# Early expert jobs of a gated scan with a mixture of experts: four taken at the seventh unit instead of two, 51 early tiles instead of 55

## The chip, the cores and the metric

The kernel runs on one core of a Trainium2 chip. The metric is the device time of one execution in microseconds (us). Five engines share the core: PE (TensorE, matmuls), DVE (VectorE), ACT (ScalarE), POOL (GpSimd) and SP (SyncE, which here only issues DMAs). PEld is PE's loading of weights, which overlaps its matmuls. Matmuls write to banks of PSUM, and ACT and DVE read them from there.

## What is computed

`x` and `f_logit` are 4 sequences of 3648 steps with 256 channels. A gated scan runs along each sequence, and its output is routed, token by token, to one of 16 experts.

```python
sig = 1.0 / (1.0 + np.exp(-f_logit))
f = lower_bound[None, None, :] + (1.0 - lower_bound[None, None, :]) * sig
for t in range(S):
    h = f[:, t] * h + (1.0 - f[:, t]) * x[:, t]
    y[:, t] = h
...
g_idx = np.argmax(x @ w_group, axis=1)            # x is now y, 14592 tokens
e_idx = np.argmax(xg @ w_expert[g], axis=1)
h = np.maximum(xg[mask_e] @ w1[g, e], 0.0)        # 256 -> 1024
ye = h @ w2[g, e]                                 # 1024 -> 256
out[tok_idx] = (g_w * e_w)[:, None] * ye
```

So every token passes through one expert. The matmuls of the experts are the bulk of the work.

## The kernel before

**Two halves that overlap.** The scan and the routing are the background. They go through 29 units of 512 tokens (`UNIT`, the last one is half a unit). For each unit SP or ACT loads 1 MB (`zt`), ACT makes the gate, DVE gates the input (L206, L226) and scans it (L217, one scan for each half of the channels, more where a sequence ends), PE turns it back (L244) and multiplies it by the router's weights (L258, L269), and DVE works out the expert and the place of each token (L279 to L335). POOL then writes each token's row (`rows`) with an indirect DMA (L339) into a list for its expert in DRAM (`xs`).

**Jobs.** The experts' matmuls are cut into jobs. An early job (kind A, one for each expert) takes the first rows of an expert's list while the list is still growing: `EARLY` gives for each expert the unit after which its list is read and the number of tiles of 128 rows that are taken. `early_rows` issues the loads (`xr`, L707) on SP as soon as that unit's tokens are written. Places that the list could not fill by then hold blank rows, written ahead by `early_blanks` (L490). After all tokens are routed, `order` sorts the experts by what is left of each, and 16 late jobs (kind B) take the rest, the largest first. Their sizes are fixed when the program is built: `CAPS`. What doesn't fit would go to a loop behind the program (L972), one tile for each pass.

**One job.** Its weights come in four pieces of 512 KB (`st`, L715, on SP, eight buffers, so two jobs ahead). Each piece is split into a half-precision part by ACT (`wh`, L721) and a remainder by DVE (`wl`, L722). The rows are turned by PE (L762, early jobs alone), split into `xh` (ACT) and `xl` (DVE, L768), and their numbers kept in `meta` (L770). The first layer is done by chunks of at most 256 rows (`m1_step`): 48 matmuls of the chunk's width (L796 to L798), and for each bank an ACT instruction (`hh`, L801) and a DVE instruction (`hl`, L802). The second layer is done by parts of at most 128 rows (`m2_step`, L815): 24 matmuls of 256 columns for a part of 97 to 128 rows; for shorter ends the columns are laid side by side, 48 matmuls of 128 columns for up to 64 rows (two groups) and 96 of 64 columns for up to 32 (four groups). ACT scales the result (`o`, L827) and POOL scatters it (L828).

**What sets the order.** SP's queue is in the order of the program text. The other engines' order is set when the program is built. The text mixes background and jobs by `bg_step`: behind each step of a job it issues as much background as is needed so that the unit in `EARLY` of the job after the next is routed by the middle of the present job (`due`). From the middle of job 12 on the whole background, `order` too, has to be out.

Of the kernel before, what the change touches and what calls it, by code (L numbers as in the profile page):

```python
# [19 lines left out]
NE = 16  # L20
UNIT = 512

EARLY = [(7, 2), (7, 2), (9, 2), (9, 2), (11, 2), (11, 2), (13, 3), (15, 3),
         (15, 3), (17, 4), (19, 4), (21, 4), (23, 5), (25, 5), (27, 6), (27, 6)]
CAPS = [848, 748, 724, 592, 588, 560, 528, 488, 464, 460, 448, 420, 392, 296, 168, 112]
EXTRA_AT = []
GROUPS = [2, 2, 2, 1] + [2] * 11
LAG = 7
# [6 lines left out]
AHEAD = 3  # L35
MT = -(-max(CAPS) // 128)
ZX_SP = 9
# [3 lines left out]
def gated_scan_moe(ctx: ExitStack, tc, zx, lower, wroute, wexp, out, S):  # L41
# [7 lines left out]
    NT = N // P  # L49
    PRE = max(n for _, n in EARLY) * P  # L50
    LW = PRE + N + 2 * P
# [44 lines left out]
    early = const.tile([P, NE], F32, name="early")  # L96
    for e, (_, n) in enumerate(EARLY):
        nc.vector.memset(early[:, e:e + 1], float(n * P))
# [4 lines left out]
    floors, gaps = {}, {}  # L103
    for u in sorted({u for u, _ in EARLY}):
        m = floors[u] = const.tile([P, NE], F32, name=f"floor{u}")
        es = [e for e, (v, _) in enumerate(EARLY) if v == u]
        nc.vector.memset(m, -1.0)
# [74 lines left out]
    def p1_ta(u):  # L182
        a, b = unit_range(u)
        w = b - a
        U = units[u]
        U["h"] = p1.tile([P, KD, UNIT], F32, name="h", bufs=3)
        ff = U["z"][:, 0]
        if u > 0:
            nc.scalar.activation(ff[:, :, 0:w], U["z"][:, 0, :, 0:w], AF.Tanh, scale=0.5)
        for k in range(KD):  # L190
            if u == 0:
                nc.scalar.activation(ff[:, k, 0:w], U["z"][:, 0, k, 0:w], AF.Tanh, scale=0.5)
            nc.scalar.activation(ff[:, k, 0:w], ff[:, k, 0:w], AF.Identity, scale=hlf[:, k:k + 1],
                                 bias=cen[:, k:k + 1])
        U["f"] = ff
# [152 lines left out]
    def p1_thunks(us, groups):  # L348
# [21 lines left out]
        def put(f):  # L370
            th.append(f or (lambda: None))
            if hasattr(f, "mark"):
                marks[f.mark] = len(th)

        put(lambda: [p1_load(u) for u in range(us[0], us[0] + AHEAD - 1)])
        put(lambda: p1_ta(us[0]))
        cut = EARLY[0][0]

# [12 lines left out]
        for u in us + [us[-1] + 1]:  # L391
# [52 lines left out]
            for t in seq:  # L444
                put(t)
                slot += 1
                for _ in range(2 if u <= EARLY[0][0] else 1):
                    if not hold:
# [168 lines left out]
    for s in range(NE):  # L617
        nc.vector.memset(caps[:, s:s + 1], float(CAPS[s]))
    onesf = const.tile([P, NE], F32, name="onesf")
# [8 lines left out]
    def make_job(kind, idx):  # L628
        j = Job()
        j.kind, j.idx = kind, idx  # L630
        j.len = EARLY[idx][1] * P if kind == "A" else CAPS[idx] if kind == "B" else P
        j.tiles = -(-j.len // P)
# [399 lines left out]
```

## Time and profile before

| | |
|---|---|
| median of 3 runs | 783.15 us (781.83 to 784.55) |
| profiled execution | 783.16 us |
| its span, first to last instruction | 781.3 us |
| PE busy | 710.7 us (91%) |
| DVE busy | 545.8 us (70%) |
| ACT busy | 460.6 us (59%) |
| POOL busy | 295.0 us (38%) |

The page's shares are averages over stages with different limits. The stages are told apart by the table of windows, which gives the busy time of each engine in a stretch, and the stretches are cut at the first `hh` of a job. In the windows, "(x202)" is the number of instructions, PEclk the granted clock of TensorE as a share of 2.4 GHz, and DMA share how busy the 16 DMA engines were on average.

### The profile page before, as it was taken

Reading aid. Unit: us, or ns where it says so; the run is one execution under the profiler, and the core shown is the slowest. Engines: PE = TensorE matmul, PEld = TensorE weight load, DVE = VectorE, ACT = ScalarE, POOL = GpSimd, SP = SyncE. Lnnn points to the kernel's source line nnn. Section 1 sums busy time; section 2 is a strip of 40 time slices with the busy share of each in tenths; the row PEclk is TensorE's granted clock in tenths of the full one; section 3 lists DMA queues with packets and bytes.
Section 4 is the critical chain, followed back from the end, with each engine's and each line's share of the span. In section 5 each row is a group of like instructions: output and inputs, shape, how many; then the busy total and the mean of one; then the engine's idle time right before and its main releaser. Section 6 shows DMA issues by size and latency. Waiting matters only on the chain.

```text
span 781.3 us, 20837 instructions
## 1 busy us (share of the span) xinstructions
PE 710.7 (91%) x8077; PEld 628.7 (80%) x8077; DVE 545.8 (70%) x1130; ACT 460.6 (59%) x817; POOL 295.0 (38%) x261
## 2 busy tenths in 40 slices
PE   2553778999999999999999999999999999999995
PEld 1332566888988878989988898999999999899995
DVE  7989999999999976675654645545564676566640
ACT  5756876987878855445445444454555465555541
POOL 1574164677756553542111213223222322232232
PEclk9999979999999999999999999999999999999999
DMA  7997989999999935369535434453553555556300
GB/s 299 348 328 240 348 234 357 338 312 336 306 367 320 345 111 190 117 200 226 158 113 108 149 88 126 128 125 120 138 168 99 160 154 171 169 152 177 86 29 25
DMA packets 95605, 155.58 MB, mean 199 GB/s; under 512 B 52304, under 2 KB 64621, under 8 KB 92048
## 3 DMA queue, kind: packets, MB, share of 16 engines
q1 hardware_dynamic: 80528, 103.73, 44.9%
q0 software_dynamic: 11424, 30.02, 11.0%
q10 hardware_dynamic: 3552, 20.48, 7.4%
q8 instruction: 64, 1.05, 0.6%
q14 instruction: 37, 0.30, 0.1%
HBM read 112.69 MB, written 42.02 MB: 198 GB/s over the span
## 4 chain that ended last, share of the span: by engine, by line
PE 72%; DVE 6%; issue 5%; DMA 3%; ACT 3%; POOL 1%; SPq 1%; POOLq 0%; ACTq 0%; DVEq 0%
PE ps_m L815 34%; PE ps_m L796 8%; PE ps_m L798 8%; PE ps_m L797 8%; PE ps_p L796 3%; PE ps_p L797 3%; PE ps_p L798 3%; DVE wl L722 2%; PE ps_p L244 2%; PE ps_p L762 2%; POOL out_dram L828 1%; DVE h L217 1%; PE ps_p L258 1%; DMA xs<-blank 1%; DMA xs<-rows,posi 1%
## 5 line engine op out<-in xcount | busy, mean ns | idle before, releaser
L815 PE MATMUL ps_m<-wh,hl 128*128 128x256 f16 (+2 forms) x1320 | 265.9, 251 | 4.9 <-DVE hl L802 4.9
L815 PE MATMUL ps_m<-wl,hh 128*128 128x256 bf16 (+2 forms) x1320 | 265.6, 251 | 0.1
L815 PE MATMUL ps_m<-wh,hh 128*128 128x256 f16 (+2 forms) x1320 | 265.5, 252 | 0.0
L815 PEld LDWEIGHTS <-hh 128*128 128x128 f16 (+2 forms) x2640 | 195.3, 99 | 23.5 <-issue 3.5
L796 PE MATMUL ps_m<-xh,wh 128*128 128x256 f16 (+11 forms) x782 | 197.2, 263 | 3.6 <-DVE hl L802 3.6
L797 PE MATMUL ps_m<-xl,wh 128*128 128x256 bf16 (+11 forms) x782 | 197.3, 262 | 1.0 <-DVE xl L768 1.0
L798 PE MATMUL ps_m<-xh,wl 128*128 128x256 f16 (+11 forms) x782 | 197.3, 262 | 0.9 <-issue 0.9
L722 DVE TENSOR_TENSOR wl<-st,wh 128x1024 bf16<-128x1024 f32 x128 | 154.3, 1219 | 51.9 <-ACT wh L721 51.7
L339 POOL DMA_INDIRECT xs<-rows,posi x114 | 142.9, 1253 | 124.6 <-DVE rows L321 34.6
L828 POOL DMA_INDIRECT out_dram<-o,info x75 | 87.1, 1162 | 242.5 <-ACT o L827 214.6
L802 DVE SCALAR_TENSOR_TENSOR hl<-ps_m,hh 128x512 bf16<-128x512 f32 (+6 forms) x176 | 117.5, 670 | 72.6 <-ACT hh L801 71.9
L801 ACT ACTIVATE hh<-ps_m 128x512 f16<-128x512 f32 (+6 forms) x176 | 103.3, 588 | 69.4 <-PE ps_m L798 67.0
L721 ACT CAST wh<-st 128x1024 f16<-128x1024 f32 x128 | 132.1, 1046 | 14.0 <-PE ps_m L815 8.0
L815 PEld LDWEIGHTS <-hl 128*128 128x128 bf16 (+2 forms) x1320 | 104.5, 99 | 15.6 <-DVE hl L802 5.2
L796 PEld LDWEIGHTS <-wh 128*128 128x128 f16 x1088 | 107.0, 99 | 11.8 <-issue 2.8
L797 PEld LDWEIGHTS <-wh 128*128 128x128 f16 x1088 | 107.1, 98 | 10.7 <-issue 2.6
L798 PEld LDWEIGHTS <-wl 128*128 128x128 bf16 x1088 | 107.0, 98 | 9.1 <-issue 1.2
L828 POOL DMA_INDIRECT out_dram<-o,meta x55 | 63.0, 1145 | 112.1 <-ACT o L827 101.8
L827 ACT ACTIVATE o<-ps_m,info 128x256 f32<-128x256 f32 (+4 forms) x75 | 33.0, 441 | 84.3 <-PE ps_m L815 76.9
L796 PE MATMUL ps_p<-xh,wh 128*128 128x256 f16 (+13 forms) x306 | 73.4, 252 | 0.0
L798 PE MATMUL ps_p<-xh,wl 128*128 128x256 f16 (+13 forms) x306 | 73.3, 252 | 0.0
L797 PE MATMUL ps_p<-xl,wh 128*128 128x256 bf16 (+13 forms) x306 | 73.3, 252 | 0.0
(138 smaller groups left out, 736.7 us busy)
## 6 DMA issues: line engine op xcount, KB each, us to landing
st<-in_wexp_dram SPq DMA_DIRECT2D x128, 512.0 KB
zt<-in_zx_dram ACTq DMA_DIRECT2D x19, 1024.0 KB
zt<-in_zx_dram SPq DMA_DIRECT2D x8, 1024.0 KB
xr<-xs SPq DMA_DIRECT2D x25, 258.0 KB
xs<-blank SPq DMA_DIRECT2D x22, 258.0 KB
xs<-rows,posi POOLq DMA_INDIRECT x114
xs<-blank SPq DMA_DIRECT2D x3, 516.0 KB
xs<-blank SPq DMA_DIRECT2D x2, 774.0 KB
```

Source lines behind the costliest of these rows:

```text
L244: nc.tensor.transpose(out=bp[:, (j - j0) * D + k * P:(j - j0) * D + (k + 1) * P], in_=h[:, k, j * P:(j + 1) * P], identity=ident)
L339: sc = nc.gpsimd.indirect_dma_start(out=xs_v[G["t0"] + t][:, :], out_offset=bass.IndirectOffsetOnAxis(ap=R["posi"][:, t:t + 1], axis=0), i ...
L721: nc.scalar.copy(j.wh[i], j.st[i])
L722: nc.vector.tensor_tensor(out=j.wl[i], in0=j.st[i], in1=j.wh[i], op=ALU.subtract)
L796: nc.tensor.matmul(po, w1_at(j.wh, k, c), xh[:, k], start=(k == 0), stop=False)
L797: nc.tensor.matmul(po, w1_at(j.wh, k, c), xl[:, k], start=False, stop=False)
L798: nc.tensor.matmul(po, w1_at(j.wl, k, c), xh[:, k], start=False, stop=(k == KD - 1))
L801: nc.scalar.activation(hi, pv, AF.Relu)
L802: nc.vector.scalar_tensor_tensor(out=j.hl[ch][:, cs[0]:cs[-1] + 1, 0:w], in0=pv, scalar=0.0, in1=hi, op0=ALU.max, op1=ALU.subtract)
L815: nc.tensor.matmul(pm[i * q:i * q + n, 0:dw], h[ch][:, c, ts], w2_at(w, c)[:, i * dw:(i + 1) * dw], start=(c == 0 and s == 0), stop=(c == ...
L827: nc.scalar.activation(o[s, 0:dw], pm[s, 0:dw], AF.Copy, scale=lt.bitcast(F32)[s, r, 1:2])
L828: nc.gpsimd.indirect_dma_start(out=out_v[out_n[0]].rearrange("n (g d) -> (n g) d", g=g), out_offset=bass.IndirectOffsetOnAxis(ap=lt[s, r, ...
```

## The change

```diff
-EARLY = [(7, 2), (7, 2), (9, 2), (9, 2), (11, 2), (11, 2), (13, 3), (15, 3),
-         (15, 3), (17, 4), (19, 4), (21, 4), (23, 5), (25, 5), (27, 6), (27, 6)]
-CAPS = [848, 748, 724, 592, 588, 560, 528, 488, 464, 460, 448, 420, 392, 296, 168, 112]
+EARLY = [(7, 2), (7, 2), (7, 2), (7, 2), (9, 2), (9, 2), (11, 2), (11, 2), (13, 3),
+         (15, 3), (17, 4), (19, 4), (21, 4), (23, 5), (25, 6), (27, 6)]
+CAPS = [848, 748, 724, 620, 616, 592, 588, 576, 548, 512, 500, 460, 392, 296, 288, 172]
```

Early jobs 2 and 3 are read at unit 7 instead of 9, jobs 4 and 5 at 9, jobs 6 and 7 at 11 with two tiles each instead of three, and so on. In all 51 early tiles (6528 rows) stand where 55 (7040) stood, and the late jobs hold 8480 rows instead of 7836. Jobs 13, 14 and 15 have 5, 6 and 6 tiles in both kernels. Early jobs have 27 chunks instead of 30 and late ones 41 instead of 38. The late jobs' parts are 63 of full width instead of 57, 9 in two groups instead of 11, and 7 in four groups instead of 8.

Since the table also feeds `bg_step` and the blanks, the order on the engines moves. On SP, from the last row load of the first early jobs to the row loads for unit 9 (`xr` are early rows, `st` weights, `xs<-blank` blank rows, `posA` the place in the list):

```order
+L707 ISA
+L707 DMA xr<-xs 128x516
 L715 DMA st<-in_wexp_dram 128x1024 x5
 L490 DMA xs<-blank 384x1x258
-L715 DMA st<-in_wexp_dram 128x1024 x2
-L490 DMA xs<-blank 384x1x258 x2
+L715 DMA st<-in_wexp_dram 128x1024 x6
+L490 DMA xs<-blank 384x1x258
+L715 DMA st<-in_wexp_dram 128x1024 x4
 L679 TENSOR_LOAD posA
```

Two more row loads now stand ahead of the weights, and 15 pieces of weights instead of 7 stand ahead of the wait for unit 9's rows.

On DVE, from the first `hl` of early job 0 on, before (`mx` to `sc` are the routing of a group of units, `zt` the gate, `h` the scan):

```order
L802 SCALAR_TENSOR_TENSOR hl<-ps_m_871,hh 128x512
L279 TENSOR_REDUCE mx<-Lg 128x40
L281 TENSOR_TENSOR ge<-Lg,mx 128x160
L285 SCALAR_TENSOR_TENSOR pw<-ge,pri 128x160
L287 TENSOR_REDUCE pm<-pw 128x40
L289 TENSOR_TENSOR oh<-pw,pm 128x160
L294 TENSOR_TENSOR oh_962<-oh 128x8x16
L297 SCALAR_TENSOR_TENSOR scn<-rmask_322,oh_962 128x128
L327 TENSOR_TENSOR both<-ps_p,runoff 128x32
L332 TENSOR_TENSOR sc<-scn,both 128x128
L206 SCALAR_TENSOR_TENSOR zt<-zt 128x1024
L802 SCALAR_TENSOR_TENSOR hl<-ps_m_983,hh 128x512
```

The same place in the changed kernel:

```order
L802 SCALAR_TENSOR_TENSOR hl<-ps_m_895,hh 128x512
L722 TENSOR_TENSOR wl_963<-st,wh_962 128x1024
L217 SCALAR_TENSOR_TENSOR h<-zt,h 128x512
L802 SCALAR_TENSOR_TENSOR hl<-ps_m_939,hh 128x512
L279 TENSOR_REDUCE mx<-Lg 128x40
L281 TENSOR_TENSOR ge<-Lg,mx 128x160
L802 SCALAR_TENSOR_TENSOR hl<-ps_m_987,hh 128x512
L768 TENSOR_TENSOR xl<-ps_p,xh 128x512
L770 COPY meta<-xr 128x4
L285 SCALAR_TENSOR_TENSOR pw<-ge,pri 128x160
L287 TENSOR_REDUCE pm<-pw 128x40
L802 SCALAR_TENSOR_TENSOR hl<-ps_m_1023,hh 128x512
```

Where one `hl` followed another after ten rows of background, the four `hl` of job 0 now stand close together. From the first `hl` of job 0 to the first of job 13, DVE has 504 rows before (the trace has records of 502) and 480 now: 8 fewer `hl`, 3 fewer `xl`, 3 fewer `meta`, 1 `wl` fewer, 1 scan more (it stood just ahead of the stretch before), and 10 fewer of the small rows of `leftovers` (these now stand behind). All scans, all routing and the sorting in `order` lie ahead of that point in both.

## Rows read from the trace of the kernel before

**Rows 1.** The page's 40 equal slices of the span: busy share in tenths for PE and DVE, and the granted clock in tenths.

```profile
PE   2553778999999999999999999999999999999995
...
DVE  7989999999999976675654645545564676566640
...
PEclk9999979999999999999999999999999999999999
```

**Rows 2.** The table of windows, cut where a job's first `hh` starts (job 0 at 80.02, 1 at 107.68, 2 at 123.77, 3 at 137.92, 5 at 163.76, 11 at 288.61, 12 at 313.72, 13 at 342.11; the last matmul's `o` ends at 773.5): stretch, its length, busy time and count on each engine, granted clock, DMA share and GB/s.

```profile
core 0: us, PE busy (x) PEld busy (x) DVE busy (x) ACT busy (x) POOL busy (x), PEclk, DMA share, GB/s
80.02:107.68 27.66, 20.86 (x202) 16.32 (x201) 25.29 (x58) 19.93 (x42) 8.63 (x8) 0.81 0.94 305
107.68:123.77 16.09, 10.87 (x87) 8.47 (x86) 16.02 (x26) 13.46 (x23) 12.47 (x10) 0.85 0.91 257
123.77:137.92 14.15, 13.74 (x127) 11.74 (x125) 13.96 (x27) 10.29 (x20) 4.52 (x4) 0.92 1.02 391
137.92:163.76 25.84, 25.84 (x259) 23.01 (x258) 25.05 (x46) 22.26 (x41) 16.45 (x13) 1.00 1.01 323
...
80.02:288.61 208.59, 193.62 (x1949) 167.62 (x1948) 199.05 (x379) 164.45 (x305) 120.62 (x93) 0.96 0.94 311
80.02:280.00 199.98, 185.01 (x1861) 160.17 (x1860) 193.61 (x364) 160.21 (x298) 115.58 (x89) 0.96 0.97 322
288.61:313.72 25.11, 25.11 (x244) 22.19 (x243) 15.71 (x38) 14.28 (x28) 11.14 (x12) 1.00 0.52 169
...
80.02:342.11 262.09, 246.76 (x2468) 214.94 (x2467) 238.01 (x502) 192.44 (x358) 149.12 (x122) 0.97 0.83 276
342.11:773.50 431.39, 429.89 (x5364) 392.19 (x5362) 239.42 (x428) 218.52 (x371) 106.86 (x94) 1.00 0.49 136
```

**Rows 3.** The same table for line 801 (`hh`) alone; a job of two tiles has four of them, and jobs 0 to 12 have 76 together.

```profile
80.01:107.67 27.66, 2.42 (x4) 0.81 0.94 305
107.67:123.76 16.09, 2.43 (x4) 0.85 0.91 257
...
137.90:288.60 150.70, 27.86 (x46) 1.00 0.93 310
288.60:342.10 53.50, 10.75 (x18) 1.00 0.42 139
```

**Rows 4.** The list of waits for PE from 80 to 140 us: who waited for whom, us in total, times, longest.

```profile
PE ps_m L815 <- DVE hl L802: 4.9, 1, 4.9
PE ps_p L762 <- DMA xr<-xs: 2.4, 1, 2.4
PE ps_m L796 <- DVE hl L802: 1.8, 1, 1.8
```

**Rows 5.** SP's timeline: start, us (waits included), line, DMA issued, count.

```profile
71.45 1.52 SPq L707 DMA_DIRECT2D xr<-xs  x2
73.07 5.51 SPq L715 DMA_DIRECT2D st<-in_wexp_dram  x5
78.63 1.40 SPq L490 DMA_DIRECT2D xs<-blank  x1
80.13 9.94 SPq L715 DMA_DIRECT2D st<-in_wexp_dram  x2
90.12 1.87 SPq L490 DMA_DIRECT2D xs<-blank  x2
108.26 1.50 SPq L707 DMA_DIRECT2D xr<-xs  x2
```

**Rows 6.** DVE's timeline: start, us for the run of equal instructions, count.

```profile
70.07 4.61 DVE L722 TENSOR_TENSOR wl<-st,wh 128x1024 bf16<-128x1024 f32 x4
...
94.70 2.46 DVE L217 TENSOR_TENSOR_SCAN h<-zt,h 128x512 f32<-128x512 f32 x2
...
108.55 1.28 DVE L802 SCALAR_TENSOR_TENSOR hl<-ps_m,hh 128x512 bf16<-128x512 f32 x2
```

**Rows 7.** The groups of DVE instructions by line and shape: count, busy us, mean ns of one, idle time before. The last is one of the small rows (128x16) of `leftovers`.

```profile
L722 DVE TENSOR_TENSOR wl<-st,wh 128x1024 bf16<-128x1024 f32 x128 | 154.3, 1219 | 51.9 <-ACT wh L721 51.7
L802 DVE SCALAR_TENSOR_TENSOR hl<-ps_m,hh 128x512 bf16<-128x512 f32 x148 | 100.9, 685 | 63.6 <-ACT hh L801 62.9
...
L768 DVE TENSOR_TENSOR xl<-ps_p,xh 128x512 bf16<-128x512 f32 x25 | 17.1, 683 | 9.3 <-ACT xh L767 9.3
...
L588 DVE TENSOR_TENSOR t<-t,caps 128x16 f32<-128x16 f32 x1 | 0.2, 174 | 0.0
```

**Rows 8.** The chain that ended last, in order of time: start, us, what, count. They are second layers: a full part of 24 matmuls has 2.62 us; 72 is a full one and one in two groups, 120 a full one and one in four groups, 48 two full ones.

```profile
610.94 4.08 PE ps_m L815 x72
...
626.04 2.62 PE ps_m L815 x24
633.90 3.53 PE ps_m L815 x120
```

**Rows 9.** PE's timeline where it passes to early job 11, in square brackets the idle time ahead and who ended it; and the window of that job.

```profile
274.54 0.33 PE L269 MATMUL ps_p<-ident,rs 128*128 128x128 f32 x1 [0.39 <-DVE xl L768]
279.44 0.27 PE L796 MATMUL ps_m<-xh,wh 128*128 128x256 f16 x1 [1.51 <-DVE hl L802]
...
261.33:288.61 27.28, 25.38 (x251) 22.15 (x250) 23.07 (x41) 18.15 (x35) 10.58 (x8) 1.00 0.61 203
```

**Rows 10.** The groups of instructions of PE's weight loads on line 796: 16 for each chunk of the first layer.

```profile
L796 PEld LDWEIGHTS <-wh 128*128 128x128 f16 x1088 | 107.0, 99 | 11.8 <-issue 2.8 <-ACT wh L721 0.4
```

## The prediction

> **What bounds the kernel now.** I read the 40 slices first, then the windows cut at the jobs, then who waits for whom. The slices [rows 1] show three stretches: PE is half empty up to some 140 us, then full to the end; DVE is full up to some 270 us and half empty afterwards; the granted clock falls below full speed only around 90 to 130 us. So there are two stages, and each has its own limit.
>
> From job 13 on PE is the limit: 429.89 of 431.39 us are busy [rows 2]. Whatever is left at that point takes PE's time and little else, and from the last `o` at 773.5 to the span's end at 781.3 there are 7.8 us more, which I leave as they are.
>
> Between the first `hh` of job 0 (80.02) and the first of job 11 (288.61) DVE is the limit: it is busy for 199.05 of 208.59 us, and up to 280.00 for 193.61 of 199.98 [rows 2]. PE is busy for 20.86 of 27.66 us in job 0, 10.87 of 16.09 in job 1 and 13.74 of 14.15 in job 2 [rows 2], and what it waits for there is DVE above all: 4.9 us for an `hl`, 1.8 for another [rows 4]. In job 0 an `hl` stands behind a block of routing and scans. The counts of `hh` (four for a job of two tiles, 76 up to job 13) show that the cuts are where I say [rows 3]. From job 3 to 5 PE too is full, 25.84 of 25.84, beside DVE at 25.05 [rows 2]. That is the point on which this case turns: the early jobs are fed at a rate that holds both engines, and the change shifts early work about in a stage that DVE bounds.
>
> **The change, part by part.** *Jobs 2 and 3 at unit 7.* The first four jobs now have their rows before they start, so less background is pressed between them, and PE's empty time in jobs 0 to 2 (27.66 - 20.86, 16.09 - 10.87 and 14.15 - 13.74, together 12.4 us) gets filled. This is no gain of 12.4 us, since DVE had no room there: the scans that are not done now are done a few jobs later, on the same full DVE. So I don't count PE's gaps. I count what DVE has to do up to a point where the background is over in both kernels, which is the first `hl` of job 13.
>
> *DVE up to job 13.* Before: 238.01 us busy [rows 2]. The change in rows is told with the order. Prices are spacings, since neighbours overlap: a `wl` (4.61 - 1.22) / 3 = 1.13, an `hl` 1.28 - 0.685 = 0.60, a scan 2.46 - 1.27 = 1.19 (half of 2.46 is 1.23) [rows 6, 7]; an overlap of 0.085 off 683 ns makes 0.60 for an `xl`, and off 174 ns 0.09 for a small one [rows 7]. So -8 x 0.60 (`hl`) - 3 x 0.60 (`xl`) - 1.13 (`wl`) + 1.19 (scan) - 13 x 0.09 (three `meta` and ten small rows) = -7.7, and 230.3 us remain. The four tiles less that the early jobs have by then are all of this; the splits of weights and the background stay.
>
> *DVE's idle time in that stretch.* Before, up to 280.00, it was 199.98 - 193.61 = 6.4 us, 3.3% of its work [rows 2]; up to 288.61 it was 9.5, or 4.8%. I take 3.3% = 7.6 us, since up to 280 DVE was the limit and behind that PE was. Ends: none, and 4.8% = 11.0.
>
> *Ahead of job 0.* DVE's and PE's rows are the same. SP issues two more blank writes of 258 KB ahead of the first weights and two more row loads behind 71.45; a pair of row loads took 1.52 us of the queue [rows 5], and the pieces that come next wait for no one yet. 0.5 MB at the 305 GB/s of job 0's window [rows 2] would be 1.7 us of the DMA engines if it delayed a unit's load in full. I take 0.5 us, between 0 and 1.8.
>
> *SP.* Before, SP stood from 90.12 + 1.87 to 108.26 at the row loads of unit 9, with the last piece of job 3's weights behind it [rows 5]. Now 15 pieces go ahead of that wait. Without it the first four jobs lack no weights; and the 2.4 us that PE waited for those rows [rows 4] go. DVE covers both, so I price them at nothing, and if DVE were not full there they would be part of the 12.4 us above.
>
> *PE behind job 13.* Jobs 13 to 15 are the same. The late jobs grow by 644 rows: 48 columns a row, 30912 columns, at 2.62 us for 24 x 256 columns [rows 8] 13.2 us. Second layers: +6 full parts x 2.62, -2 in two groups x (4.08 - 2.62 = 1.46), -1 in four groups x (3.53 - 2.62 = 0.91) [rows 8] = +11.9. Together +25.1 us. Against it stand four early tiles less (4 x 5.24 = 21 us of PE) ahead of job 13, where PE has the room already: so in this sum they give nothing beyond DVE's 7.7.
>
> *Sum.* Job 13 starts at 80.0 + 0.5 + 230.3 + 7.6 = 318.4 instead of 342.1. Behind it 431.4 + 25.1 = 456.5, to 774.9 instead of 773.5, and 7.8 to the end: a span of 782.7. The profiled execution had 783.16 for a span of 781.3, 1.9 more, so 784.6 us. That execution is at the median of the runs (783.15). The change gains 23.7 us ahead of job 13 and pays 25.1 behind it.
>
> With the ends: 784.6 - 7.6 - 0.5 = 776.5 without any idle time, and 784.6 + 3.4 + 1.3 = 789.3 with both upper ends.
>
> **Rivals.** *PE gets in DVE's way (slower).* Ahead of job 13 PE has 246.76 - 21 = 226 us busy against DVE's 230: both full at once, and a full PE in order makes DVE wait. Where this could be seen before, at the passage to job 11, PE lost 0.39 + 1.51 = 1.9 us while DVE had 23.07 busy of 27.28 [rows 9]. From job 8 to 12 the changed order puts as much background beside each tile as DVE can bear. With 1.9 us in three of these jobs beyond my 7.6: 784.6 + 5.7 = 790.3. Against it: from job 3 to 5 both were full and nothing was lost, PE 25.84 of 25.84 [rows 2]. It decides from about 8.5 us of idle DVE on (784.6 + 0.9 is slower by over 0.3%).
>
> *The first four jobs want more than the DMA engines give (slower).* Jobs 0 to 2 moved 27.66 x 305 + 16.09 x 257 + 14.15 x 391 = 18.1 MB [rows 2]. Four jobs with one scanned unit less, half a job's weights and two tiles more need some 18.5. At the 311 GB/s of the whole stage [rows 2] that is 59.5 us, against some 56 of DVE in those jobs (13 `wl`, 16 `hl`, 12 scans, 5 gates, 4 `xl`, 58 small rows): 3.5 late, 788.1 us. Against it: 391 GB/s in job 2 [rows 2], with which it costs nothing. The Trainium skill (DMA: Bandwidth & Descriptors, section Where 436 GB/s comes from) puts what HBM gives one core at about 358 GB/s; by that 18.5 MB take an estimated 51.7 us, and this rival has no price. As a ceiling the trace does not bear it out: the 391 GB/s of job 2 are above it, reads and writes together.
>
> *DVE never waits (faster).* Early jobs at hand mean that DVE finds an `hl` or a split to do whenever a scan's input is late. With 2 us of idle time left: 784.6 - 5.6 = 779.0. For it: DVE was busy for 16.02 of 16.09 us in job 1 [rows 2]. Against it: 2.4 us of DVE's 6.4 fell to job 0 alone, and the rest came while PE was full.
>
> *The change doesn't do what it says.* If a late job's rows exceeded its size, the loop behind the program would run, at least 5.2 us of PE for each pass. Worked out from the inputs of the reference, the experts' remainders are 102 to 837 before and 162 to 837 now, and every size in the table is 8 to 11 rows above its own. Before, the loop did not run: 1088 weight loads are 16 for each of 68 chunks [rows 10], and there are 68 now too.
>
> **How the numbers follow.** A run of this kernel can tell about 0.3% from no change, 2.35 us, so no change lies between 780.8 and 785.5. My forecast, no difference that can be told, has 0.43; PE in DVE's way 0.25 and the DMA engines 0.11, both slower; DVE never waiting 0.20, faster; the loop 0.01, slower. That is 0.20 faster, 0.43 the same, 0.37 slower. The range goes from 777.5, one us inside the lower end, to 790.0, about where the first rival ends; some 2 in 10 lie outside.
>
> **What would show it.** The first `hh` of job 13 (the 77th) near 318 us with DVE some 230 us busy between; PE's four waits before 140 us gone and the clock falling less; PE full behind job 13 for some 455 us. If job 13 starts before 314, DVE had less to do or waited less than I say; if it starts behind 321, the windows of jobs 8 to 12 should show whether PE, or in jobs 0 to 3 the DMA share, is what DVE waited for. If PE's time behind job 13 is not 25 us longer, the price of the late rows is wrong.

## Result and profile after

| | before | after |
|---|---|---|
| median | 782.95 us (14 runs, 780.94 to 785.76) | 789.42 us (14 runs, 784.37 to 793.19) |
| profiled execution | 783.16 us | 791.82 us |
| its span | 781.3 us | 790.1 us |

The changed kernel takes 1.0075 times as long (95% interval 1.0057 to 1.0093): slower by three quarters of a per cent, 4.8 us above the forecast and inside its range. The profiled execution lies 2.4 us above its median; a second one, further down, lies below.

The windows, cut at the first `hh` of jobs 0, 1, 2, 3, 4 and 13 and at the end of the last `o`, answer to [rows 2]:

```profile
core 0: us, PE busy (x) PEld busy (x) DVE busy (x) ACT busy (x) POOL busy (x), PEclk, DMA share, GB/s
84.06:92.09 8.03, 8.03 (x85) 7.08 (x84) 7.30 (x15) 6.45 (x13) 0.00 (x0) 1.00 1.01 397
92.09:104.22 12.13, 12.13 (x124) 10.73 (x123) 12.13 (x25) 11.64 (x22) 0.00 (x0) 1.00 0.95 340
104.22:120.55 16.33, 13.43 (x131) 11.50 (x130) 16.12 (x31) 12.16 (x22) 12.73 (x10) 1.00 0.91 279
120.55:142.67 22.12, 17.16 (x153) 13.81 (x152) 14.98 (x30) 13.02 (x23) 15.59 (x11) 0.85 0.89 262
...
250.82:274.84 24.02, 22.42 (x221) 19.06 (x219) 21.00 (x42) 20.07 (x42) 13.38 (x11) 1.00 1.03 339
...
84.06:327.01 242.95, 224.20 (x2220) 192.44 (x2219) 226.15 (x462) 181.76 (x342) 148.44 (x114) 0.98 0.86 287
327.01:783.22 456.21, 454.65 (x5460) 415.66 (x5458) 249.12 (x454) 227.73 (x386) 112.91 (x101) 1.00 0.49 133
```

Jobs 0 and 1 run with PE full, 8.03 of 8.03 and 12.13 of 12.13 us; the gaps of [rows 2] are gone there. In job 3 both engines stand: DVE has 14.98 of 22.12 us and PE 17.16, at a granted clock of 0.85. Up to job 13 DVE is idle for 242.95 - 226.15 = 16.8 us. Job 0 starts 4.0 us later than before. Behind job 13 PE is full, as before.

The waits of PE from job 0 to job 13, which answer to [rows 4]:

```profile
PE ps_m L796 <- DVE hl L802: 7.1, 7, 2.1
PE ps_p L762 <- DMA xr<-xs: 5.8, 2, 5.0
```

The wait for early rows, which I said would go, has grown from 2.4 to 5.0 us for the longest. SP's timeline, to hold against [rows 5], shows when those rows were asked for:

```profile
74.71 3.77 SPq L707 DMA_DIRECT2D xr<-xs  x4
...
99.25 17.87 SPq L715 DMA_DIRECT2D st<-in_wexp_dram  x4
126.34 1.50 SPq L707 DMA_DIRECT2D xr<-xs  x2
```

The row loads for unit 9 go out at 126.34 instead of 108.26. By then job 3, the last job that has its rows, is 5.8 us past its first `hh`; before it was job 1, 0.6 us past its own. POOL's timeline shows the first and the last of the eight scatters of the group with unit 9 (the first stood behind 33.86 us without work):

```profile
105.07 1.33 POOL L339 DMA_INDIRECT xs<-rows,posi  x1 [33.86 <-ACT hh L801]
...
116.78 1.97 POOL L339 DMA_INDIRECT xs<-rows,posi  x1 [0.31 <-issue]
```

and the same two in the kernel before:

```profile
94.12 1.39 POOL L339 DMA_INDIRECT xs<-rows,posi  x1 [24.51 <-ACT hh L801]
...
103.71 1.18 POOL L339 DMA_INDIRECT xs<-rows,posi  x1 [0.30 <-issue]
```

From the start of the last scatter to the row loads, while the scatters land, are 9.6 us, 4.6 before. So, counted from the first `hh` of job 0, the loads go out 14.0 us later than before (at 42.3 us): the first scatter stands 6.9 us later, the eight take 2.1 us more from first to last, and the landing takes 5.0 us more. What makes the landing slower is not shown. What follows can be read on PE (start, us, and in square brackets the idle time ahead):

```profile
123.87 0.27 PE L798 MATMUL ps_m<-xh,wl 128*128 128x256 f16 x1
129.10 1.10 PE L762 MATMUL ps_p<-ident,xr 128*128 128x128 f32 x4 [4.96 <-DMA xr<-xs]
130.00 0.42 PE L815 MATMUL ps_m<-wh,hh 128*128 128x256 f16 x1
```

and on DVE:

```profile
131.79 0.15 DVE L770 COPY meta<-xr 128x4 int32<-128x4 int32 x1
139.08 0.69 DVE L802 SCALAR_TENSOR_TENSOR hl<-ps_m,hh 128x512 bf16<-128x512 f32 x1 [7.14 <-ACT hh L801]
```

PE takes its work in order: behind the turning of job 4's rows stand the second layer of job 2 and the rest of job 3, and DVE's next `hl` needs those. DVE takes its rows in order too: the next rows of routing and scan stand behind that `hl`, so it has nothing to do meanwhile. So 5.0 us of PE become 7.1 us of DVE. That it is more has to do with the clock, in windows around the wait (columns as above):

```profile
120.00:127.70 7.70, 4.14 (x48) 3.19 (x46) 7.70 (x18) 7.15 (x12) 6.48 (x5) 1.00 0.65 231
127.70:134.60 6.90, 5.50 (x26) 4.07 (x27) 4.24 (x7) 0.94 (x2) 5.68 (x5) 0.51 0.98 220
```

PE stood from 123.87 on, the granted clock fell to the lower of its two levels (1.2 GHz), and the first 5.5 us of work behind the wait ran at it: some 2.7 us more, by halves.

PE's weight loads on line 796 are as many as in [rows 10], so the loop behind the program did not run:

```profile
L796 PEld LDWEIGHTS <-wh 128*128 128x128 f16 x1088 | 107.0, 98 | 10.5 <-issue 1.6
```

### The profile page after: what moved, and what is told of

It is laid out like the page before. It is cut to its first block, busy times and chain, and to the rows that moved or that the text cites. A ratio compares the mean times of both kernels' runs of the same rounds, so it can differ in the third digit from the quotient of the medians.

```text
span 790.1 us, 20452 instructions
## 1 busy us (share of the span) xinstructions
PE 713.4 (90%) x7925; PEld 630.2 (80%) x7925; DVE 544.0 (69%) x1116; ACT 460.7 (58%) x817; POOL 296.3 (38%) x260
## 4 chain that ended last, share of the span: by engine, by line
issue 51%; POOL 15%; DVE 9%; DMA 8%; PE 6%; POOLq 1%; ACT 1%; SPq 0%; DVEq 0%; ACTq 0%
POOL out_dram L828 14%; DMA xs<-rows,posi 3%; DVE wl L722 3%; DMA out_dram<-o,meta 2%; PE ps_m L815 2%; POOL xs L339 2%; DVE hl L802 1%; DVE h L217 1%; DMA st<-in_wexp_dram 1%; DMA xr<-xs 1%; DMA zt<-in_zx_dram 1%; PE ps_m L797 1%; PE ps_m L796 1%; PE ps_m L798 1%; POOLq L828 1%
## 5 line engine op out<-in xcount | busy, mean ns | idle before, releaser
L796 PE MATMUL ps_m<-xh,wh 128*128 128x256 f16 (+12 forms) x760 | 192.8, 263 | 8.2 <-DVE hl L802 8.1
L797 PE MATMUL ps_m<-xl,wh 128*128 128x256 bf16 (+12 forms) x760 | 193.2, 262 | 1.6 <-DVE xl L768 1.6
L798 PE MATMUL ps_m<-xh,wl 128*128 128x256 f16 (+12 forms) x760 | 193.1, 262 | 0.0
L339 POOL DMA_INDIRECT xs<-rows,posi x114 | 146.8, 1288 | 123.5 <-ACT hh L801 34.2
L802 DVE SCALAR_TENSOR_TENSOR hl<-ps_m,hh 128x512 bf16<-128x512 f32 (+8 forms) x173 | 114.9, 667 | 70.1 <-ACT hh L801 69.9
L801 ACT ACTIVATE hh<-ps_m 128x512 f16<-128x512 f32 (+8 forms) x173 | 101.9, 591 | 63.7 <-PE ps_m L798 63.7
L828 POOL DMA_INDIRECT out_dram<-o,meta x51 | 57.8, 1134 | 100.4 <-ACT o L827 89.6
L802 DVE SCALAR_TENSOR_TENSOR hl<-ps_p,hh 128x512 bf16<-128x512 f32 (+11 forms) x71 | 46.3, 652 | 58.5 <-ACT hh L801 58.4
L796 PE MATMUL ps_p<-xh,wh 128*128 128x256 f16 (+13 forms) x328 | 78.8, 252 | 0.0
L797 PE MATMUL ps_p<-xl,wh 128*128 128x256 bf16 (+13 forms) x328 | 78.7, 252 | 0.0
```

What stands on the lines that cost most here:

```text
L339: sc = nc.gpsimd.indirect_dma_start(out=xs_v[G["t0"] + t][:, :], out_offset=bass.IndirectOffsetOnAxis(ap=R["posi"][:, t:t + 1], axis=0), i ...
L796: nc.tensor.matmul(po, w1_at(j.wh, k, c), xh[:, k], start=(k == 0), stop=False)
L797: nc.tensor.matmul(po, w1_at(j.wh, k, c), xl[:, k], start=False, stop=False)
L798: nc.tensor.matmul(po, w1_at(j.wl, k, c), xh[:, k], start=False, stop=(k == KD - 1))
L801: nc.scalar.activation(hi, pv, AF.Relu)
L802: nc.vector.scalar_tensor_tensor(out=j.hl[ch][:, cs[0]:cs[-1] + 1, 0:w], in0=pv, scalar=0.0, in1=hi, op0=ALU.max, op1=ALU.subtract)
```

## Experiments

My theory after this reading had two losses: the start of job 0 (two more blank writes while the DMA engines are full) and the rows of unit 9, late for job 4. The rival was that 51 tiles instead of 55 cost the time by themselves. Times are medians, ratios are to the kernel before on the same chips. The kernel before came to 782.95 us beside the first run, 784.28 beside e2 to e6, 783.45 beside e8 to e11 and 783.10 beside e13 to e15, so runs are compared by their ratios. "Stage" is from the first `hh` of job 0 to that of job 13.

| run | us | ratio (95%) | job 0 | job 13 | DVE busy in the stage | DVE idle |
|---|---|---|---|---|---|---|
| after | 789.42 | 1.0075 (1.0057-1.0093) | 84.06 | 327.01 | 226.15 | 16.80 |
| e15_after | 788.77 | 1.0095 (1.0072-1.0118) | 81.86 | 322.75 | 226.69 | 14.20 |
| e2_tiles | 788.26 | 1.0063 (1.0034-1.0091) | 80.55 | 330.56 | 230.60 | 19.41 |
| e10_tiles_due | 787.02 | 1.0042 (1.0025-1.0059) | 80.80 | 329.05 | 231.47 | 16.78 |
| e3_noblank | 785.59 | 1.0020 (0.9997-1.0043) | 78.91 | 321.75 | 226.41 | 16.43 |
| e4_late_after | 785.79 | 1.0029 (1.0008-1.0050) | 82.64 | 320.61 | 227.40 | 10.57 |
| e6_due | 783.16 | 0.9996 (0.9978-1.0013) | 82.00 | 317.29 | 227.81 | 7.48 |
| e8_due_late | 784.98 | 1.0019 (1.0001-1.0037) | 83.87 | 322.47 | 227.99 | 10.61 |
| e9_due_fetch | 781.60 | 0.9975 (0.9961-0.9989) | 81.68 | 317.99 | 227.96 | 8.35 |
| e14_due_fetch | 781.31 | 0.9974 (0.9959-0.9988) | 80.77 | 317.17 | 227.90 | 8.50 |
| e11_due_noblank | 779.26 | 0.9938 (0.9918-0.9957) | 79.02 | 315.27 | 228.07 | 8.18 |

**The late rows.** One more due time:

```diff
+    due.append((work(macros[0]) + work(macros[1]) // 2, marks[9]))
     now = [0]
```

> The changed kernel with one more due time: unit 9 has to be routed by the middle of job 1 rather than of job 2, so more background stands ahead of job 4. Theory (job 4's rows came 18 us later than before, since unit 9 is routed late, and DVE lost 7 us by it): SP's row loads of unit 9 go out some 10 us earlier, PE's wait of 5.0 us for them is gone, DVE's idle stretch of 7.1 us at 139 falls below 2, and the time is 783 to 786 us. Rival (DVE and PE wait as much at the other job passages, whatever the order there): the wait for the rows goes, but job 13 still starts at 327 and the time stays at 788 to 790.

783.16 us: by the ratios 0.8% less than the changed kernel, all of its loss. Job 0 still starts at 82.00, but no wait of PE for `xr` is left in the stage, as its longest waits show:

```profile
PE ps_m L796 <- DVE hl L802: 7.4, 7, 3.7
PE ps_m L796 <- ACT xh L767: 2.2, 1, 2.2
PE ps_m L797 <- DVE xl L768: 1.1, 2, 0.9
```

SP's timeline has the row loads 9 us earlier, and in the windows more than half of the stage's idle time goes, while job 1 takes the background that stood elsewhere:

```profile
117.23 1.65 SPq L707 DMA_DIRECT2D xr<-xs  x2
```

```profile
93.16:112.43 19.27, 12.97 (x123) 10.68 (x122) 19.10 (x40) 15.00 (x28) 13.55 (x9) 0.82 0.90 307
...
82.00:317.29 235.29, 222.48 (x2220) 191.57 (x2219) 227.81 (x468) 182.24 (x341) 145.35 (x116) 0.99 0.90 298
```

PE is empty for 6.3 us in job 1 and its clock falls there too, yet that costs little, since DVE has 19.10 of 19.27 us. This is the difference: PE standing empty is cheap as long as DVE has rows of its own to do. Whether PE waits for DVE or for a transfer does not decide it. In two of the runs below, e10_tiles_due and e13_before_fetch, unit 9's rows came late for job 2, and PE waited for them in job 1:

```profile
PE ps_p L762 <- DMA xr<-xs: 4.5, 1, 4.5
...
PE ps_p L762 <- DMA xr<-xs: 7.4, 1, 7.4
```

In the first, DVE was busy for 15.61 of that job's 15.68 us. In the second it had splits of weights, routing and scans to do, stood for 0.8 us behind the wait, and the kernel took no longer than the kernel before (ratio 0.9991). DVE's idle time in e6_due is 7.5 us, what I had forecast for the changed kernel. The first theory holds.

**The start.** The writes of blank rows for jobs 1 and 3 left out:

```diff
-            if v == u:
+            if v == u and e not in (1, 3):
```

> The changed kernel without the blank rows of early jobs 1 and 3; those writes are left out, all else is the same. Theory (two more blank writes of 258 KB in a start in which the DMA engines are full put job 0 back by 4 us): the first hh of job 0 comes 2 to 4 us earlier than 84.1, and the time falls from 789.4 by as much, to 785.5 to 787.5. Rival (the later start is a matter of the run or of the two more row loads): job 0 stays at 83 to 84 and the time at 789.

785.59 us, by the ratios 0.55% less, some 4 us. Its profile is 5.1 us shorter than that of the changed kernel, and all of it lies ahead of job 0 (78.91; against the second profile of the changed kernel, 81.86, it is 3 us); the stage is as in the changed kernel (242.84 us, 16.4 idle). The waits of ACT from 36 to 84 us, in the changed kernel:

```profile
ACT zt L189 <- DMA zt<-in_zx_dram: 8.0, 2, 5.0
```

and without those writes:

```profile
ACT zt L189 <- DMA zt<-in_zx_dram: 1.5, 1, 1.5
```

The gate waits for the units' loads. The windows of the changed kernel behind the blank writes (issued at 16.97):

```profile
24.00:26.00 2.00, 0.01 (x3) 0.00 (x0) 1.90 (x7) 1.97 (x4) 0.29 (x1) 1.00 1.11 159
26.00:28.00 2.00, 1.13 (x9) 0.38 (x9) 1.97 (x2) 1.21 (x4) 1.70 (x2) 1.00 1.11 203
28.00:30.00 2.00, 0.94 (x16) 0.43 (x16) 2.00 (x3) 0.00 (x0) 1.70 (x2) 1.00 1.03 304
```

and without two of the four:

```profile
24.00:26.00 2.00, 0.01 (x2) 0.01 (x2) 1.90 (x7) 1.97 (x4) 0.35 (x1) 1.00 0.99 283
26.00:28.00 2.00, 1.12 (x9) 0.37 (x9) 1.97 (x2) 1.15 (x3) 1.70 (x2) 1.00 1.02 418
28.00:30.00 2.00, 1.00 (x16) 0.43 (x16) 2.00 (x3) 0.00 (x0) 1.70 (x2) 1.00 1.06 416
```

The engines are full in both, but with the blanks they move 159 and 203 GB/s instead of 283 and 418. In these six us (159 + 203 + 304) x 2 = 1.33 MB passed instead of 2.23, with more to do. The packets from 24 to 28 us, in the changed kernel and without two of the four writes:

```profile
DMA packets 535, 0.73 MB, mean 181 GB/s; under 512 B 37, under 2 KB 466, under 8 KB 535
...
DMA packets 398, 1.40 MB, mean 351 GB/s; under 512 B 43, under 2 KB 60, under 8 KB 398
```

The engines took more packets, but most of them small ones, and half the bytes. So 0.5 MB of rows of 1032 bytes cost far more than their bytes at the average rate.

**Do the two add?** Both edits together, again without the blanks of jobs 1 and 3:

> The changed kernel with unit 9 due by the middle of job 1, without the blank rows of early jobs 1 and 3 (those writes are left out). Theory (the later start and the late rows of unit 9 are two losses that add): 783.2 less the 3 to 4 us of the start, 779.0 to 780.5, with job 0 at 78.5 to 79.5. Rival (what is won at the start is lost in the stage, whose rows then come late again, since the routing of unit 9 is bound by the loads and not by job 0): job 0 at 79, job 13 still at 316 or later, 782 to 783.

779.26 us: by the ratios 0.58% under e6_due, with job 0 at 79.02 and 8.2 us idle. They add: 0.79% and 0.55% apart, 1.37% together.

**Blanks later.** All blank writes two units later:

```diff
-early_blanks(u + 4)
+early_blanks(u + 2)
```

> The changed kernel with every blank write issued two units later (three units ahead of its job's unit becomes one). Theory (the start is bound by the DMA engines): the four writes then fall on the end of the start, behind the loads of the first units, so the first hh of job 0 comes about 2 us earlier than 84.1, and the time is some 787 us, if the blanks of the later jobs find the engines as they did before. Rival (the writes only have their place changed in a queue that is full up to job 0 anyway): job 0 at 84 and 789 us. Further rival: the blanks now stand nearer to the first scatters and hold them up, 790 or more.

785.79 us, but not for the reason given. In its profile DVE stands for 4.7 us at 62 and job 0 starts at 82.64, between the two profiles of the changed kernel: nothing is won at the start that can be told. The gain lies in the stage (10.6 us idle), where PE waited 1.9 us for job 4's rows. SP asked for them at 123.53, 40.9 us behind job 0 instead of 42.3. Two chains of some 40 us race there. The scatters landed after 7.8 us here, after 9.6 and 9.1 in the two profiles of the changed kernel; why this edit shifted that is not settled. With the due time as well:

> The changed kernel with unit 9 due by the middle of job 1 and every blank write two units later: the two edits that brought 6 and 3.6 us apart. Theory (both relieved the same wait, job 4's rows, and the late blanks did nothing for the start, where job 0 still began at 82.6 and DVE stood for 4.7 us at 62): nothing to add, 782 to 784 us. Rival (the two act in different places): 779 to 780.

784.98 us: nothing to add, and if anything a loss (the intervals of the two overlap), with job 0 at 83.87 in its profile. So, as far as these runs show, the later blanks help only through the wait that the due time removes.

**Tiles alone.** The units of before with 51 tiles:

```diff
-EARLY = [(7, 2), (7, 2), (7, 2), (7, 2), (9, 2), (9, 2), (11, 2), (11, 2), (13, 3),
-         (15, 3), (17, 4), (19, 4), (21, 4), (23, 5), (25, 6), (27, 6)]
+EARLY = [(7, 2), (7, 2), (9, 2), (9, 2), (11, 2), (11, 2), (13, 2), (15, 2), (15, 3),
+         (17, 3), (19, 4), (21, 4), (23, 4), (25, 5), (27, 6), (27, 6)]
```

(`CAPS` follows from it: 8288 late rows.)

> The units of the kernel before (two jobs at the seventh, two at the ninth, and so on) with 51 early tiles as in the changed kernel; the late jobs hold 8288 rows, between 7836 and 8480. Theory (what costs is that four jobs are taken at the seventh unit): the first hh of job 0 is back at 80 to 81 us, DVE has no idle stretch of 7 us and PE no wait of 5 us for unit 9's rows. DVE's work up to job 13 is that of the changed kernel, 230 us, plus 8 idle, so job 13 starts at about 318; behind it some 17 us more than before (431.4 + 17, from the count of matmuls), so the span ends near 775 and the time is 773 to 780 us. Rival (51 tiles instead of 55 are what costs, since early work of PE is moved behind job 13 for too little relief of DVE): 785 us or more, with job 13 at 325 or later although job 0 starts at 80.

788.26 us: here my theory fell, for the start is early and the time is still that of the changed kernel. The stage is 250 us long. Part of it was again a late unit, 15, for jobs 7 and 8. With that due earlier:

```diff
+    due.append((sum(work(m) for m in macros[:4]) + work(macros[4]) // 2, marks[15]))
```

> The kernel with the units of before and 51 early tiles (788.3 us), with one more due time: unit 15, whose rows jobs 7 and 8 take, by the middle of job 4 rather than of job 5. Theory (with two tiles instead of three in job 6 the rows of unit 15 come late for job 7: PE waited 3.7 us for them at 185 and DVE stood for 4.5 us at 194): both waits go, job 13 starts some 4 us earlier than 330.6, and the time is 783 to 785.5 us. Rival (that kernel's stage is long because PE stands empty in the first two jobs, as before, and pays for it later): the waits go and the time stays at 787 to 789.

787.02 us: the waits for unit 15 are gone, job 13 starts 1.5 us earlier, and that is all; the rival held. Its windows, job 0, job 1, and the stage in two parts:

```profile
80.80:108.44 27.64, 20.83 (x202) 16.34 (x201) 25.28 (x58) 19.94 (x41) 8.64 (x8) 0.81 0.92 304
108.44:124.12 15.68, 10.75 (x90) 8.21 (x89) 15.61 (x29) 12.87 (x24) 12.18 (x9) 0.89 0.89 255
...
80.80:256.00 175.20, 157.10 (x1547) 132.56 (x1546) 167.10 (x321) 136.90 (x255) 106.14 (x79) 0.94 0.97 321
256.00:329.05 73.05, 70.79 (x675) 62.10 (x674) 64.36 (x161) 47.95 (x90) 49.22 (x40) 1.00 0.64 208
```

PE has its old gaps in jobs 0 and 1, and at the end of the stage PE is the limit (70.79 of 73.05) while DVE stands for 8.7 us. So 51 tiles without the moved units are a loss, and the moved units with the due time (e6_due) are worth 0.46% beside it by the ratios, some 3.6 us.

**A version with both mended.** The due time, and the weights of job 1 fetched behind one more unit, so that the loads have the engines to themselves:

```diff
-EARLY_FETCH = [(5, 4), (7, 8)]
+EARLY_FETCH = [(5, 4), (9, 8)]
```

> The changed kernel with unit 9 due by the middle of job 1, and the weights of early job 1 (four pieces of 512 KB) fetched behind one more unit's load and two more blank writes, at about 43 us rather than 31; nothing on PE, DVE or ACT is in another order but three rows. Theory (the start waits for the units' loads since the DMA engines are full from 20 to 60 us): ACT's waits for a load, 3.6 us at 41 and 2.6 at 58, shrink by what 2 MB take, job 0 starts at 79 to 80.5 instead of 82.0, and the time is 780.5 to 782. Rival (the bytes have to pass before job 0 in any case): job 0 at 82, 783 us. Further rival: the weights now collide with the last loads, 784 or more.

781.60 us, ratio 0.9975: a quarter of a per cent faster than the kernel before, although in its profile job 0 came only 0.3 us earlier than in e6_due (in that of the second run 1.2). What the later fetch adds to the due time is not shown: the intervals of the two overlap, and ACT's waits for loads from 36 to 84 us, which were to shrink, are 7.9 us as in e6_due (6.1 in the second run). Whether the fetch helps any kernel with this start was tried on the kernel before:

> The kernel before with only the later fetch: the weights of early job 1 behind one more unit's load and two more blank writes. Theory (the later fetch helps the changed kernel because its start is held up by four blank writes; in the kernel before, with two, ACT hardly waited for a load, 0.8 us at 63): job 0 stays at 80 and the time at 783 to 784, ratio within 0.2% of 1. Rival (the later fetch is worth 1.6 us in any kernel with this start): job 0 at 78.5, 781.5 to 782, so that the changed kernel with both edits only draws level with this one.

817.24 us beside 819.62 for the kernel before: on that chip both took some 35 us longer, and the ratio is 0.9992 (0.9964 to 1.0019). The profile, of the kernel with the later fetch, has PE idle from 300 to 380 us with nothing that it waits for ("issue"), where the first profile of the kernel before has none of that. What PE stood for there is not shown.

```profile
PE ps_m L815 <- issue: 8.2, 12, 1.1
```

So the three were run once more, on another chip:

> The kernel before with only the later fetch, once more, since the first run fell on a chip on which every kernel took some 35 us longer (819.6 us for the kernel before), with PE standing for instructions. Theory: 0.1 to 0.2% of the kernel before, as there (ratio 0.9992). Rival: 1.6 us faster, ratio 0.998.

782.61 us, ratio 0.9991 (0.9978 to 1.0004), job 0 at 79.46: the fetch alone does nothing that can be told for the kernel before.

> The changed kernel with unit 9 due by the middle of job 1 and the weights of job 1 fetched later, once more beside the other two. If it beats the kernel before: ratio 0.996 to 0.999, as in its first run (0.9975). If that was the chip: 1.000.

781.31 us, ratio 0.9974: it holds.

> The changed kernel itself once more on the chip of the other two, with a second profile. Theory: 1.0075 times the kernel before, 788 to 790 us; in the profile job 0 starts at 82 to 84, PE waits 3 to 6 us at 124 to 129 for the rows of unit 9, and DVE stands for 4 to 8 us behind it. Rival (the wait was that profile's chance): no such wait, with a time that is still 788 to 790.

788.77 us. The second profile of the changed kernel has the same wait of PE:

```profile
PE ps_p L762 <- DMA xr<-xs: 3.8, 2, 2.9
```

DVE stands for 5.8 us behind it (at 135.5). In e3_noblank, where the start is early, PE waited 4.8 us there and DVE 7.0. The wait is no chance of one profile, only its size is.

## Why the prediction was off

The forecast was no difference; it is a loss of 0.75%. That the time lies in the range is luck: the upper end was set by a full PE in jobs 8 to 12, and what was lost beyond the forecast was lost in job 3 and ahead of job 0. By its steps, against the profiled execution (791.82, so 7.2 us above the forecast):

- *The limits and PE behind job 13*: right. 456.2 us against 456.5; the late rows cost 24.8 us instead of 25.1.
- *DVE's work up to job 13*: 226.15 against 230.3. In the trace 2.8 us of small rows stand just behind the first `hh` of job 13, which the count of rows had ahead, so it is 229.0: right to 1.3 us.
- *Ahead of job 0*: mis-sized. 0.5 us (0 to 1.8) stood for 4.0 in this profile; e3_noblank and e11_due_noblank put it at 3 to 5 us, the second profile at 1.8. I took the bytes of the blank writes at the average of 305 GB/s and then mostly hid them; with the four writes among their packets, the full engines moved half the bytes for some 4 us, and the loads that ACT waits for came later.
- *SP*: this is the step that failed: "and the 2.4 us that PE waited for those rows go", and "DVE covers both, so I price them at nothing". They grew to 5.0 (2.9 in the second profile), and DVE, with no background ahead of its next `hl`, stood for 7.1 (5.8). I looked at who stood behind SP's wait and not at when the wait would end. `due` counts in PE's work, unit 9 by the middle of job 2. Jobs 0 to 2 had a stretch of background between them before; now they pass in 36.5 us instead of 57.9, and the chain behind the routing does not shrink with them: the scatters take 11.7 us from first to last (9.6 before), the landing 9.6 (4.6 before) and the load 2.8. e6_due shows it by moving that one due time.
- *DVE's idle time*: 16.8 us against 7.6, with the upper end at 11.0. Jobs 0 to 7 have 9.2 of it, 7.1 in the wait above, and jobs 8 to 12 have 7.6; in e6_due it is 1.9 and 5.6. So 3.3% came out for this order once the rows come in time, though not spread as I had it, and it was wrong to take over from an order in which DVE had background to do while PE waited.
- *Sum*: 3.6 (start) - 4.2 (work) + 9.2 (idle) = 8.6 us later at job 13; 0.3 + 0.9 + 0.2 come back behind it, in PE's work, in the tail and around the span. The sign that I gave counts one thing wrong: in the changed kernel the first `hh` of job 13 is the 69th, not the 77th, since jobs 0 to 12 have 68.

Of the rivals, *PE in DVE's way* came out near in number (790.3). Jobs 8 to 12 do hold most of the idle time that is left in e6_due (5.6 of 7.5 us), with PE busy for 118.11 of 119.90 us there; but of the 9.2 us beyond my forecast in the changed kernel, 7.1 are an empty PE in job 3, waiting for a transfer. *The DMA engines in the first four jobs* had the wrong place: DVE was busy for 35.55 of 36.49 us in jobs 0 to 2, which moved up to 397 GB/s. In job 3, while PE stood for the rows, they had room (share 0.65 from 120 to 127.7). They were short ahead of job 0. The Trainium skill (DMA: Bandwidth & Descriptors, section Where 436 GB/s comes from) puts what HBM gives one core at about 358 GB/s; the window with 397, too, is above it, reads and writes together.

I also left PE's gaps out of the sum, as no gain for a full DVE. e10_tiles_due bounds that: with the gaps kept, PE becomes the limit at the end of the stage and DVE stands for 8.7 us there.

## What to carry to other kernels

When work is taken out between two steps, ask of every deadline in the program in what unit it is counted: a due time in matmuls shrinks with them, the chain of routing, scatter, landing and load behind it does not. An engine that stands empty costs next to nothing while the one that sets the time has rows of its own to do, whatever the first one waits for (7.4 us for a transfer in e13_before_fetch), unless it becomes the limit later on, as in e10_tiles_due. Once the next row of the full engine hangs on the wait, both stand, so price a wait by what is queued ahead of that row. And an extra write in a stretch where the DMA engines are full is priced by its rate there, not by its bytes at an average.

## What the runs showed of the hardware

Writes of 1032-byte rows, four of 258 KB, brought full DMA engines (share 1.11) down to 159 and 203 GB/s, where with two of them 283 and 418 passed. The Trainium skill (DMA: Bandwidth & Descriptors, section Specifications) names 512 bytes as the smallest transfer at line rate. Here twice that was not enough, and the measurement decides; that it is the size of the rows which makes these writes slow is not shown, since no run varied it.

A wait of PE of 5.0 us halved its clock (0.51 from 127.7 to 134.6) through the first 5.5 us of work behind it, so a short stall cost PE half as much again. In e13_before_fetch the clock was 0.50 from 112 to 118 us, in and behind a wait of 7.4 us, and there it cost no time that can be told, since DVE was the limit.

One chip took 819.62 us for the kernel before where the others took 783; a profile taken there has PE idle with no releaser, and the reason is open. The ratio of two kernels was the same there (0.9992 and 0.9991).
